# Attention with V split in two: both halves of V in one 32-column stationary operand, two passes per split step in place of three

## Chip, core and metric

The kernel runs on one core of a Trainium2 chip. The metric is device time in microseconds (us) of one execution. "Before" has a median of 1079.02 us over three runs (1078.17 to 1079.59).

## What is computed

Input x has 2048 rows of 512. Two branches are mixed row by row with a gate g = sigmoid(x · gate_w):

```python
q = (x @ wq) as 32 heads of 16;  k = x @ wk;  v = x @ wv      # one k and one v of 16 columns for all heads
a = softmax(q @ k.T / 4) @ v, heads joined, @ wo              # wo: 512 x 512
b = silu(x @ w1) @ w2                                         # w1: 512 x 1792, w2: 1792 x 512
out = g * a + (1 - g) * b
```

All of it is asked for in fp32. The kernel gets there with 16-bit products: a number is held as a high half and a low half (fp16 or bf16), and a product is the sum of three 16-bit products, or it is done natively in fp32.

## The kernel before, in words

**Prologue** (`first_pass`, L351 to L489). x is transposed on TensorE and split; k, v, and the first queries are computed. `VF` (L484) holds V in fp32 with 16 dims and a column of ones (column 16, for the softmax sum) in 32 columns per tile of 128 keys. `v_parts` (L332) makes `VH` (fp16 of V) and `VL` (V minus VH). After it, in VectorE's order, come a minimum (`note`, L349), the low half of the second query block (L117), and then the work of the first step of attention. PSUM banks 6 and 7 are the buffers `pm` of the products between.

**Attention** (`attention`, L701). A round is 512 queries (chunk c), an output block o of 128 query columns and a half rb: 32 rounds. A step is one tile of 128 keys of a round: 16 steps per round, 512 in all. The loop (L1067) takes two steps, a pair, at a time, and issues a pair's work in an order written out as a string: `SPLIT`, `NATIVE` or their wide forms (L27).

- **S** (`scores`, L987): eight small matmuls (32 columns each) write scores into a two-bank PSUM tile; there are two of these tiles. Then ScalarE does one exp over 128x1024 (L1000). A step has two S, a pair four.
- **F**: eight matmuls of other products, the feed-forward, the projection of the output or queries (L741), which fill the array. A pair has 6 F, a wide one 12.
- **P** or **N** (`pv`, L1026): probabilities times V, of earlier steps. The even step of the pair before comes as three P (`VH`·upper half, `VL`·upper half, `VH`·lower half) where it is split, or as one native fp32 N. The odd step is always N. In the program a P is 8 matmuls and an N stands in the profile as 16.
- **low** (`low`, L1010): for a split step VectorE takes the upper half (a bf16 view of the fp32 bits) off the probabilities, two instructions of 128x1024 (L1021). They are issued at the third and fourth S of the step's own pair, so before the P that reads them by about a pair. Step 0 of each round and steps under some feed-forward phases are native (`split_step`, L1006).
- **norm_a** (L939): after a round's last N the accumulators pv0 and pv1 (one buffer each) are transposed into T and U, added, and divided by column 16. It goes to VectorE's queue ahead of whatever the next pair issues. `norm_b` and `norm_c` (L952, L956) finish a pair of rounds, and `out_proj` uses the result.
- **The planner** (`spend`, `put`, `fill`, L750 to L779): each pair has room for 3.7 us of VectorE work (4.1 or 4.95 in two cases). Work that cannot be moved is booked with `spend` (1.15 per low, 2.4 for a norm_a, 0.68 for an eviction of a product); what can wait (norm_b at 0.65, the split of a hidden block at 1.0, pieces of weights at 1.3, maxima at 1.1) is issued at the end of a pair if it fits in what is left, or when it is due by age.

After the last pair the remaining products run (L1106 on). The last output projection waits for the last round's norm_a, norm_b and norm_c.

**Ranges** (`RANGES`, L39): maxima of the operands are compared with limits; if one lies outside, a second, scaled pass of the whole work follows (L1115).

Of the kernel before, what the change touches and what calls it, by code (L numbers as in the profile page):

```python
# [6 lines left out]
F32 = mybir.dt.float32  # L7
BF = mybir.dt.bfloat16
F16 = mybir.dt.float16
# [4 lines left out]
OP = mybir.AluOpType  # L14
AX = mybir.AxisListType
# [6 lines left out]
NF = max(GF)  # L22
ACCS = 4

SPLIT, NATIVE = "SFFFSFFFSPPPSBN", "SFFFSFFFSNBSN"  # L27
WIDE = {SPLIT: "SFFFFFFSFFFFFFSPPPBSN", NATIVE: "SFFFFFFSFFFFFFSNBSN"}

FIRST = "EEEEEEEEEESEESEEEESEEEESBEEEE"  # L30
AHEAD, EARLY = 2, (4, 5)
# [5 lines left out]
QS = LAM / KS  # L37

RANGES = ((0, 8, 0.5, 7.8), (8, 16, 0.5, 7.8), (16, 23, 1.0, 6e4), (23, 25, 1.0, 6e4), (25, 26, 1.0, 6e4),  # L39
          (26, 27, 1.0, 6e4), (27, 28, 1.0, 6e4), (28, 29, 1.0, 6e4), (29, 30, 1.0, 6e4),  # L40
          (30, 31, -1.0, LIMIT * LAM / ONE), (31, 32, -1.0, 0.5))
M_X, M_1, M_2, M_O, M_Q, M_K, M_V, M_G, M_VV, M_B, M_KK = (r[0] for r in RANGES)

# [2 lines left out]
def kernel(  # L46
# [21 lines left out]
    nc = tc.nc  # L68
# [5 lines left out]
    NKT = S // 128  # L74
# [5 lines left out]
    consts = ctx.enter_context(tc.tile_pool(name="consts", bufs=1))  # L80
# [1 line left out]


    KT = consts.tile([128, S], F16)
    VH = consts.tile([128, NKT, 32], F16)
    VL = consts.tile([128, NKT, 32], F16)
    VF = consts.tile([128, NKT, 32], F32)
    gg = consts.tile([128, NKT], F32)
    g1 = consts.tile([128, NKT], F32)
    xs = consts.tile([128, 2, KD, S], F16)  # L90
# [114 lines left out]
    nc.gpsimd.memset(mxs, 0.0)  # L205
    for q in qb_:
        nc.gpsimd.memset(q, 0.0)
    for t_ in (VH, VL, VF):
        nc.gpsimd.memset(t_, 0.0)
    nc.gpsimd.memset(VH[:, :, 16:17], 1.0)  # L210
    nc.gpsimd.memset(VF[:, :, 16:17], 1.0)

    def masks(cst):
        jp = cst.tile([128, 128], F32)
# [50 lines left out]
    def scales(pool, psum, e, srcs, targets):  # L265

        n = len(targets)
        pt_ = psum.tile([128, 512], F32, name="pk")
        nc.tensor.transpose(pt_[0:n, 0:128], srcs, ident)
        m = pool.tile([8, 1], F32, name="am")  # L270
        nc.vector.tensor_reduce(m[0:n], pt_[0:n, 0:128], axis=AX.X, op=OP.max)
        power(m[0:n], m[0:n])
        d = pool.tile([8, 8], F32, name="ad")
        nc.vector.tensor_scalar(d[0:n, 0:n], ident[0:n, 0:n], m[0:n], None, op0=OP.mult)
        one = pool.tile([8, 128], F32, name="one")
        nc.vector.memset(one, 1.0)
# [52 lines left out]
        nc.vector.tensor_scalar(gg, gg, 1.0, None, op0=OP.add)  # L329
        nc.vector.reciprocal(gg, gg)  # L330

    def v_parts():  # L332
        nc.vector.tensor_copy(VH[:, :, 0:16], VF[:, :, 0:16])
        nc.vector.tensor_tensor(VL[:, :, 0:16], VF[:, :, 0:16], VH[:, :, 0:16], op=OP.subtract)


    qsc = QS / (SX * SQ)
# [13 lines left out]
    def first_pass():  # L351
        with ExitStack() as pro:
            sb = pro.enter_context(tc.tile_pool(name="pro", bufs=1))
            wk_ = pro.enter_context(tc.tile_pool(name="prow", bufs=2))
            ps = pro.enter_context(tc.tile_pool(name="props", bufs=1, space=PSUM))
# [126 lines left out]
            V(2)  # L482
            V(3)
            nc.vector.tensor_copy(VF[:, :, 0:16], pv_[:, :, 0:16])  # L484
            v_parts()
            note()
            for _ in q1:
                pass
# [12 lines left out]
    def second_pass():  # L501
        with ExitStack() as pro:
            sb = pro.enter_context(tc.tile_pool(name="pro", bufs=1))
            wk_ = pro.enter_context(tc.tile_pool(name="prow", bufs=2))
            ps = pro.enter_context(tc.tile_pool(name="props", bufs=2, space=PSUM))
# [10 lines left out]
            for a in range(8):  # L516
                n, h = a // 2, a % 2 * F // 2
# [66 lines left out]
            scales(sb, ps, ev, vm, (2.0 ** 13,))  # L584
            nc.vector.tensor_scalar(VF[:, :, 0:16], pv_[:, :, 0:16], ev[:, 0:1], None, op0=OP.mult)
            v_parts()
# [114 lines left out]
    def attention(ctx, scale_of, t_scale, shifts, split_pieces, chores, q_todo, bounds, early, gates_):  # L701
# [237 lines left out]
        def norm_a(pv, rb, st):  # L939

            T, U = wp.tile([128, 512], F32, name="T"), wp.tile([128, 512], F32, name="U")
            T3, U3 = (t.rearrange("p (a b) -> p a b", b=32) for t in (T, U))
            nc.vector.transpose(T, pv[0])  # L943
            nc.vector.transpose(U, pv[1])  # L944
            nc.vector.tensor_tensor(T3[:, :, 0:17], T3[:, :, 0:17], U3[:, :, 0:17], op=OP.add)  # L945
            r = wp.tile([128, 16, 1], F32, name="rr")
            nc.vector.reciprocal(r, T3[:, :, 16:17])
            if rb == 0:
                st["C"] = wp.tile([128, 16, 32], F32, name="C")
            nc.vector.tensor_tensor(st["C"][:, :, 16 * rb:16 * rb + 16], T3[:, :, 0:16], r.to_broadcast([128, 16, 16]), op=OP.mult)  # L950
# [28 lines left out]
        probs, lows, lq, native = {}, {}, [], set()  # L979
# [43 lines left out]
        def upper(P):  # L1023
            return P.bitcast(BF).rearrange("p h (n two) -> p h n two", two=2)[:, :, :, 1]

        def pv(s, n):  # L1026

            i, k = steps[s]
            if k == 0 and n in (0, 3):
                pvs[i] = [pO.tile([128, 512], F32, name=f"pv{h}") for h in range(2)]  # L1030
            first, last = k == 0 and n in (0, 3), k == NKT - 1
            if n == 3:
                a, b = VF[:, k], probs.pop(s)
            else:
                while n == 2 and lq and lq[0][1] == s:
                    low(*lq.pop(0))
                a = (VH, VL, VH)[n][:, k]
                b = lows.pop(s) if n == 2 else upper(probs[s])
                if n == 2:
                    probs.pop(s)  # L1040
            for j in range(4):
                for h, r in enumerate((lo, hi_)):
                    nc.tensor.matmul(pvs[i][h][32 * j:32 * j + 32], a[r], b[r, j], start=first, stop=last)  # L1043
# [23 lines left out]
        for s in range(0, len(steps) + 2, 2):  # L1067
            on = s < len(steps)
            ending[0] = not on
            if on and steps[s][1] == 0:  # L1070
                i = steps[s][0]
                prefetch(i + 1)
                if q_todo and i % 2 == 0:
                    queue.append(q_todo.pop(0))
            p, more = 2 * s, True
            slots, order = SPLIT, [(s - 2, 0), (s - 2, 1), (s - 2, 2), (s - 1, 3)]
# [68 lines left out]
```

## Time and profile before

| what | value |
|---|---|
| three runs | 1078.17, 1079.02, 1079.59 us |
| profiled execution, first to last instruction (span) | 1075.3 us |
| what lies around the span, against the median of the runs | 3.7 us |
| VectorE busy in 300 to 560 / 820 to 1050 us | 201.21 of 260 / 159.38 of 230 us |
| granted TensorE clock | 0.998 |
| split steps / native steps | 174 / 338 |

The profile page gives no time of its own for the profiled execution besides the span; the 3.7 us are taken as the same for both kernels. Split steps are the 1392 matmuls of one of the three P groups divided by eight, native steps the 5408 fp32 records divided by sixteen. Busy time of TensorE is not a measure of what is left in it, since matmuls overlap and their ends are modelled: the distance between the starts of two passes is. A timeline row gives start, duration, engine, line, operation, tiles, shapes and a count of merged instructions, and in brackets the idle time before it with what ended it.

### The profile page before, as it was taken

The page shows a single profiled execution, that of the slowest core. Times are in us where ns is not written, and L with a number is a line of the kernel's source. Part 1 is how long each engine was busy: PE and PEld are TensorE (multiplying, and loading weights), DVE is VectorE, ACT ScalarE, POOL GpSimd, SP SyncE. Part 2 cuts the span into 40 slices and gives each one's busy share as a digit, 9 for nine tenths or more (in the row PEclk, how much of TensorE's full clock was granted, in tenths as well). Part 3 has the DMA queues.
Part 4 walks back from the last instruction along what each step waited for, and adds up shares of the span by engine and source line. Part 5 has one row for each costly group of instructions (what it writes and reads, how often), then busy time and mean ns, then how long its engine had stood idle before and what let it go on. Part 6 is the DMA issues. An engine that isn't in the chain of part 4 may idle for free.

```text
span 1075.3 us, 65967 instructions
## 1 busy us (share of the span) xinstructions
PE 1057.2 (98%) x31224; PEld 667.5 (62%) x31224; DVE 789.9 (73%) x1082; ACT 1008.6 (94%) x1121; POOL 23.4 (2%) x53
## 2 busy tenths in 40 slices
PE   8999999999999999999999999999999999999996
PEld 5455776766665577677655568677756555555552
DVE  6856986968778786878777697675857767476875
ACT  5799999999999999999999999899989999999992
POOL 2110000000000000000000000000000000000000
PEclk9999999999999999999999999999999999999999
DMA  5311111220001000000000100000000110000001
GB/s 208 115 61 45 49 42 31 61 60 14 11 11 41 32 22 10 17 12 12 22 11 21 37 19 21 22 12 11 20 6 12 31 31 12 11 11 5 11 4 43
DMA packets 20840, 32.95 MB, mean 31 GB/s; under 512 B 5137, under 2 KB 12050, under 8 KB 20562
## 3 DMA queue, kind: packets, MB, share of 16 engines
q1 hardware_dynamic: 17618, 20.46, 5.9%
q0 software_dynamic: 2512, 8.13, 2.6%
q8 instruction: 246, 4.03, 1.5%
q14 instruction: 32, 0.26, 0.1%
q10 hardware_dynamic: 432, 0.07, 0.0%
HBM read 20.12 MB, written 8.52 MB: 27 GB/s over the span
## 4 chain that ended last, share of the span: by engine, by line
PE 89%; DVE 5%; ACT 4%; issue 1%; POOL 0%; POOLq 0%; ACTq 0%
PE pv L1043 35%; PE pm L741 31%; PE S L997 19%; ACT P L1000 4%; DVE L L1021 1%; PE pm L745 1%; PE pt L311 0%; PE pk L126 0%; DVE xs L117 0%; DVE T L943 0%; PE pk L127 0%; PE pk L125 0%; DVE U L944 0%; PE pm L342 0%; DVE T L945 0%
## 5 line engine op out<-in xcount | busy, mean ns | idle before, releaser
L1000 ACT ACTIVATE P<-S 128x1024 f32<-128x1024 f32 x1024 | 963.5, 1051 | 24.6 <-PE S L997 19.4
L997 PE MATMUL S<-qb,KT 50*32 50x512 f16 x8192 | 480.1, 378 | 2.3 <-ACT P L1000 2.2
L1021 DVE TENSOR_TENSOR L<-P 128x1024 f16<-128x1024 f32 x348 | 408.1, 1217 | 8.3 <-ACT P L1000 8.2
L1043 PE MATMUL pv<-P,VF 64*32 64x512 f32 x5408 | 374.8, 589 | 0.0
L997 PEld LDWEIGHTS <-KT 50*32 50x32 f16 x8192 | 188.6, 90 | 193.9 <-issue 126.7
L741 PE MATMUL pm<-w2s,H 64*32 64x512 f16 x5232 | 258.8, 375 | 0.6 <-DVE qx L825 0.2
L741 PE MATMUL pm<-xs,w1s 64*32 64x512 f16 x5376 | 248.5, 375 | 1.1 <-issue 0.6
L741 PEld LDWEIGHTS <-H 64*32 64x32 f16 x5232 | 143.7, 93 | 43.5 <-issue 11.3
L741 PEld LDWEIGHTS <-w1s 64*32 64x32 f16 x5376 | 136.3, 93 | 46.1 <-issue 13.5
L1043 PEld LDWEIGHTS pv<-P,VF 64*32 64x32 f32 x5408 | 125.0, 107 | 30.3 <-issue 8.1
L790 DVE SCALAR_TENSOR_TENSOR e<-e,pm 128x512 f32<-128x512 f32 x56 | 38.5, 687 | 140.3 <-ACT e L789 139.4
L1043 PE MATMUL pv<-P,VH 64*32 64x512 bf16 x1392 | 81.9, 389 | 0.0
L1043 PE MATMUL pv<-L,VH 64*32 64x512 f16 x1392 | 81.4, 374 | 0.0
L1043 PE MATMUL pv<-P,VL 64*32 64x512 bf16 x1392 | 81.4, 385 | 0.0
L741 PE MATMUL pm<-xs,wqs 64*32 64x512 f16 x1152 | 81.1, 375 | 0.0
L1043 PEld LDWEIGHTS <-VH 64*32 64x32 f16 x2784 | 60.7, 92 | 20.4 <-issue 3.8
L741 PE MATMUL pm<-wo_s,O 64*32 64x512 f16 x1440 | 63.3, 375 | 0.0
L943 DVE STREAM_TRANSPOSE T<-pv 128x512 f32<-128x512 f32 x32 | 23.0, 717 | 48.0 <-PE pv L1043 40.4
L722 DVE SCALAR_TENSOR_TENSOR acc<-pm,g,acc 128x512 f32<-128x512 f32 x48 | 35.8, 745 | 26.4 <-PE pm L741 24.6
L741 PEld LDWEIGHTS <-wqs 64*32 64x32 f16 x1152 | 43.6, 93 | 10.1 <-issue 2.8
L121 DVE TENSOR_TENSOR H<-e,H 128x512 f16<-128x512 f32 x56 | 38.8, 693 | 1.9
L789 ACT ACTIVATE e<-pm 128x512 f32<-128x512 f32 x56 | 34.5, 616 | 5.7 <-PE pm L741 5.7
(155 smaller groups left out, 478.9 us busy)
## 6 DMA issues: line engine op xcount, KB each, us to landing
qb<-qd SPq DMA_DIRECT2D x192, 32.0 KB
raw<-in_B_w_dram POOLq DMA_DIRECT2D x23, 256.0 KB, 2.9
xn<-in_A_x_dram SPq DMA_DIRECT2D x8, 512.0 KB
out_dram<-acc SPq DMA_DIRECT2D x16, 256.0 KB
qd<-qx SPq DMA_DIRECT2D x12, 256.0 KB
raw<-in_A_wo_dram POOLq DMA_DIRECT2D x4, 256.0 KB, 3.6
qb<-sh SPq DMA_DIRECT2D x62, 2.0 KB
raw<-in_B_w_dram SPq DMA_DIRECT2D x3, 256.0 KB
```

What stands on the lines that cost most here:

```text
L121: nc.vector.tensor_tensor(a2, a, a1, op=OP.subtract)
L722: nc.vector.scalar_tensor_tensor(a, po, gate[:, n:n + 1], a, op0=OP.mult, op1=OP.add)
L741: nc.tensor.matmul(self.bank[32 * m:32 * m + 32], l(i, rows, 32 * m), r(j, rows), start=first, stop=last)
L745: nc.tensor.matmul(self.bank, l(i, slice(0, 128), 0, 128), r(j, slice(0, 128)), start=first, stop=last)
L789: nc.scalar.activation(e, ph, AF.Tanh, scale=t_scale)
L790: nc.vector.scalar_tensor_tensor(e, e, 1.0, ph, op0=OP.add, op1=OP.mult)
L943: nc.vector.transpose(T, pv[0])
L997: nc.tensor.matmul(sc[32 * m:32 * m + 32, f], KT[b:b + 50, k0:k0 + 32], qtile[i][b:b + 50, j], start=True, stop=True)
L1000: nc.scalar.activation(P[:, 2 * j:2 * j + 2], sc, AF.Exp, scale=scale_of(c, o))
L1021: nc.vector.tensor_tensor(lows[s][:, q], P[:, q], upper(P)[:, q], op=OP.subtract)
L1043: nc.tensor.matmul(pvs[i][h][32 * j:32 * j + 32], a[r], b[r, j], start=first, stop=last)
```

## The change

`VH` and `VL` become one operand `VP` of 32 columns. Columns 7 to 15 hold the high half of dims 7 to 15, and columns 23 to 31 their low half. Column 16 stays the ones, so dim 0 has no column for its remainder: dims 0 to 6 are rounded to a grid of 4, and what dim 0 loses is written as six base-4 digits, which are added to the grid values of dims 1 to 6 and taken off again in their low columns 17 to 22. A split step is then VP·upper and VP·lower, and norm_a puts the columns together: it adds column 16+d to column d, and dim 0 gets the sum of columns 17 to 22, each times a power of 1/4 (`mu`).

```diff
-SPLIT, NATIVE = "SFFFSFFFSPPPSBN", "SFFFSFFFSNBSN"
-WIDE = {SPLIT: "SFFFFFFSFFFFFFSPPPBSN", NATIVE: "SFFFFFFSFFFFFFSNBSN"}
+SPLIT, NATIVE = "SFFFSFFFSPPSBN", "SFFFSFFFSNBSN"
+WIDE = {SPLIT: "SFFFFFFSFFFFFFSPPBSN", NATIVE: "SFFFFFFSFFFFFFSNBSN"}
...
-    def v_parts():
-        nc.vector.tensor_copy(VH[:, :, 0:16], VF[:, :, 0:16])
-        nc.vector.tensor_tensor(VL[:, :, 0:16], VF[:, :, 0:16], VH[:, :, 0:16], op=OP.subtract)
+    def v_parts(pool):
+        n = 1 + DIGITS
...
+        nc.vector.tensor_copy(VP[:, :, n:16], VF[:, :, n:16])
+        nc.vector.tensor_tensor(VP[:, :, 16 + n:32], VF[:, :, n:16], VP[:, :, n:16], op=OP.subtract)
+        nc.vector.tensor_scalar(R, VF[:, :, 0:n], GRID * MAGIC, None, op0=OP.add)
+        nc.vector.tensor_scalar(flat_(R), flat_(R), GRID * MAGIC, None, op0=OP.subtract)
+        nc.vector.tensor_tensor(r, VF[:, :, 0:n], R, op=OP.subtract)
+        nc.vector.tensor_tensor(J, r, mu.to_broadcast([128, NKT, n]), op=OP.mult)
+        nc.vector.tensor_reduce(flat_(y), J, axis=AX.X, op=OP.add)
+        nc.vector.tensor_scalar(flat_(y), flat_(y), 1.0 / GRID, None, op0=OP.mult)
+        nc.vector.memset(J[:, :, 0:1], 0.0)
+        for d in range(1, n):
+            j = J[:, :, d:d + 1]
+            nc.vector.tensor_scalar(j, y, BASE, MAGIC, op0=OP.mult, op1=OP.add)
+            nc.vector.tensor_scalar(j, j, MAGIC, None, op0=OP.subtract)
+            if d < n - 1:
+                nc.vector.scalar_tensor_tensor(y, y, BASE, j, op0=OP.mult, op1=OP.subtract)
+        nc.vector.scalar_tensor_tensor(VP[:, :, 0:n], J, GRID, R, op0=OP.mult, op1=OP.add)
+        nc.vector.scalar_tensor_tensor(VP[:, :, 17:16 + n], J[:, :, 1:n], -GRID, r[:, :, 1:n], op0=OP.mult, op1=OP.add)
...
-            nc.vector.tensor_tensor(T3[:, :, 0:17], T3[:, :, 0:17], U3[:, :, 0:17], op=OP.add)
+            nc.vector.tensor_tensor(T, T, U, op=OP.add)
+            z = U3[:, :, 0:DIGITS]
+            nc.vector.tensor_tensor(z, T3[:, :, 17:17 + DIGITS], mu[:, :, 1:].to_broadcast([128, 16, DIGITS]), op=OP.mult)
+            nc.vector.tensor_tensor(T3[:, :, 1:16], T3[:, :, 1:16], T3[:, :, 17:32], op=OP.add)
+            nc.vector.tensor_reduce(U3[:, :, 16:17], z, axis=AX.X, op=OP.add)
+            nc.vector.tensor_tensor(T3[:, :, 0:1], T3[:, :, 0:1], U3[:, :, 16:17], op=OP.add)
...
-                while n == 2 and lq and lq[0][1] == s:
+                while n == 1 and lq and lq[0][1] == s:
...
-                a = (VH, VL, VH)[n][:, k]
-                b = lows.pop(s) if n == 2 else upper(probs[s])
+                a = VP[:, k]
+                b = lows.pop(s) if n else upper(probs[s])
...
-                spend(2.4)
+                spend(3.1)
```

Beside this: the fills of `VH` and `VL` on GpSimd at the start become one of a column of ones and seven of `mu`; the range for the largest |V| becomes 512 to 8000 (it was 1 to 60000); and in the second pass V is scaled to 2^11 rather than 2^13.

More of the change, by code (lines that the diff above doesn't have):

```diff
@@ L23 @@
 ACCS = 4
-SPLIT, NATIVE = "SFFFSFFFSPPPSBN", "SFFFSFFFSNBSN"
-WIDE = {SPLIT: "SFFFFFFSFFFFFFSPPPBSN", NATIVE: "SFFFFFFSFFFFFFSNBSN"}
+GRID, DIGITS, BASE, MAGIC = 4.0, 6, 4.0, 1.5 * 2.0 ** 23
+SPLIT, NATIVE = "SFFFSFFFSPPSBN", "SFFFSFFFSNBSN"
+WIDE = {SPLIT: "SFFFFFFSFFFFFFSPPBSN", NATIVE: "SFFFFFFSFFFFFFSNBSN"}
 FIRST = "EEEEEEEEEESEESEEEESEEEESBEEEE"
@@ L39 @@
 RANGES = ((0, 8, 0.5, 7.8), (8, 16, 0.5, 7.8), (16, 23, 1.0, 6e4), (23, 25, 1.0, 6e4), (25, 26, 1.0, 6e4),
-          (26, 27, 1.0, 6e4), (27, 28, 1.0, 6e4), (28, 29, 1.0, 6e4), (29, 30, 1.0, 6e4),
+          (26, 27, 1.0, 6e4), (27, 28, 1.0, 6e4), (28, 29, 1.0, 6e4), (29, 30, 512.0, 8000.0),
           (30, 31, -1.0, LIMIT * LAM / ONE), (31, 32, -1.0, 0.5))
@@ L84 @@
     KT = consts.tile([128, S], F16)
-    VH = consts.tile([128, NKT, 32], F16)
-    VL = consts.tile([128, NKT, 32], F16)
+    VP = consts.tile([128, NKT, 32], F16)
     VF = consts.tile([128, NKT, 32], F32)
+    mu = consts.tile([128, 1, 1 + DIGITS], F32)
     gg = consts.tile([128, NKT], F32)
@@ L207 @@
         nc.gpsimd.memset(q, 0.0)
[L208 to L211, printed above, removed]
+    nc.gpsimd.memset(VF, 0.0)
+    for t_ in (VP, VF):
+        nc.gpsimd.memset(t_[:, :, 16:17], 1.0)
+    for d in range(1 + DIGITS):
+        nc.gpsimd.memset(mu[:, :, d:d + 1], BASE ** -d if d else -1.0)
     def masks(cst):
@@ L330, in gates @@
         nc.vector.reciprocal(gg, gg)
-    def v_parts():
-        nc.vector.tensor_copy(VH[:, :, 0:16], VF[:, :, 0:16])
-        nc.vector.tensor_tensor(VL[:, :, 0:16], VF[:, :, 0:16], VH[:, :, 0:16], op=OP.subtract)
+    def v_parts(pool):
+        n = 1 + DIGITS
+        R, r, J = (pool.tile([128, NKT, n], F32, name=f"v{q}") for q in "RrJ")
+        y = pool.tile([128, NKT, 1], F32, name="vy")
+        flat_ = lambda t_: t_.rearrange("p a b -> p (a b)")
+        nc.vector.tensor_copy(VP[:, :, n:16], VF[:, :, n:16])
[15 more added lines that the diff above has]
+        nc.vector.scalar_tensor_tensor(VP[:, :, 17:16 + n], J[:, :, 1:n], -GRID, r[:, :, 1:n], op0=OP.mult, op1=OP.add)
     qsc = QS / (SX * SQ)
@@ L484, in first_pass @@
             nc.vector.tensor_copy(VF[:, :, 0:16], pv_[:, :, 0:16])
-            v_parts()
+            v_parts(sb)
             note()
@@ L583, in second_pass @@
             ev = sb.tile([128, 2], F32)
-            scales(sb, ps, ev, vm, (2.0 ** 13,))
+            scales(sb, ps, ev, vm, (2.0 ** 11,))
             nc.vector.tensor_scalar(VF[:, :, 0:16], pv_[:, :, 0:16], ev[:, 0:1], None, op0=OP.mult)
-            v_parts()
+            v_parts(sb)
             sigmoid(pv_, zsc)
@@ L1034, in pv @@
             else:
-                while n == 2 and lq and lq[0][1] == s:
+                while n == 1 and lq and lq[0][1] == s:
                     low(*lq.pop(0))
-                a = (VH, VL, VH)[n][:, k]
-                b = lows.pop(s) if n == 2 else upper(probs[s])
-                if n == 2:
+                a = VP[:, k]
+                b = lows.pop(s) if n else upper(probs[s])
+                if n:
                     probs.pop(s)
@@ L1075, in attention @@
             p, more = 2 * s, True
-            slots, order = SPLIT, [(s - 2, 0), (s - 2, 1), (s - 2, 2), (s - 1, 3)]
+            slots, order = SPLIT, [(s - 2, 0), (s - 2, 1), (s - 1, 3)]
             if s - 2 in native:
```

## The prediction, made before the changed kernel was run

> **What bounds the kernel now.** I read the engines' shares first, then the chain that ended last, then the costliest groups.
>
> ```profile
> PE 1057.2 (98%) x31224; PEld 667.5 (62%) x31224; DVE 789.9 (73%) x1082; ACT 1008.6 (94%) x1121; POOL 23.4 (2%) x53
> ...
> PE 89%; DVE 5%; ACT 4%; issue 1%; POOL 0%; POOLq 0%; ACTq 0%
> ...
> L1000 ACT ACTIVATE P<-S 128x1024 f32<-128x1024 f32 x1024 | 963.5, 1051 | 24.6 <-PE S L997 19.4
> L1043 PE MATMUL pv<-P,VL 64*32 64x512 bf16 x1392 | 81.4, 385 | 0.0
> ```
>
> TensorE (PE) is the chain, but ScalarE (ACT) stands at 94% beside it. So the question is not what a P pass takes on PE, but how far PE lies behind ACT's own pace. The timeline of PE over a split pair near the end shows the first; starts count, not durations.
>
> ```profile
> 1035.15 0.41 PE L997 MATMUL S<-qb,KT 50*32 50x512 f16 x8
> 1035.37 0.84 PE L741 MATMUL pm<-wo_s,O 64*32 64x512 f16 x24
> 1036.02 0.41 PE L997 MATMUL S<-qb,KT 50*32 50x512 f16 x8
> ...
> 1036.89 0.41 PE L997 MATMUL S<-qb,KT 50*32 50x512 f16 x8
> 1037.11 0.42 PE L1043 MATMUL pv<-P,VH 64*32 64x512 bf16 x8
> 1037.34 0.42 PE L1043 MATMUL pv<-P,VL 64*32 64x512 bf16 x8
> 1037.56 0.41 PE L1043 MATMUL pv<-L,VH 64*32 64x512 f16 x8
> 1037.78 0.41 PE L997 MATMUL S<-qb,KT 50*32 50x512 f16 x8
> ...
> 1038.86 0.41 PE L997 MATMUL S<-qb,KT 50*32 50x512 f16 x8
> ...
> 1040.49 0.41 PE L997 MATMUL S<-qb,KT 50*32 50x512 f16 x8 [0.36 <-ACT P L1000]
> ```
>
> A group of eight matmuls starts about 0.22 after the one before (three F and an S in 0.87); the N costs four (1037.78 to 1038.86 is 1.08 with its S). The pair takes 3.71 from S to S: 17 groups. The last row is of the next pair, which has one block of F less: there PE **waits 0.36 us for ACT**. So ACT's pace is close under 3.71. The timeline of ACT gives it:
>
> ```profile
> 311.59 0.60 ACT L789 ACTIVATE e<-pm 128x512 f32<-128x512 f32 x1
> 312.07 7.46 ACT L1000 ACTIVATE P<-S 128x1024 f32<-128x1024 f32 x8
> 319.34 0.68 ACT L789 ACTIVATE e<-pm 128x512 f32<-128x512 f32 x1
> 319.82 37.24 ACT L1000 ACTIVATE P<-S 128x1024 f32<-128x1024 f32 x40
> 356.94 0.61 ACT L789 ACTIVATE e<-pm 128x512 f32<-128x512 f32 x1
> ```
>
> From 312.07 to 319.34 stand eight exps without a gap: 0.909 each, **3.635 per pair**; a tanh adds 0.48 (319.34 to 319.82). The forty from 319.82 to 356.94 take 0.928 each, the pace of PE's 3.71.
>
> **The pass that goes.** A split pair falls to 16 groups, 3.71 - 0.22 = 3.49, and ACT's 3.635 takes over: 0.075 are gained, a third of the pass. The distances between first S of pairs sort them:
>
> ```profile
> L997 PE MATMUL S<-qb,KT x8192: 372/377/388, 38.8 to 1052.4; 50*32 50x512 f16 x200
> ```
>
> Of 256 pairs, 172 in the loop are split. Of the 152 with six F whose exps I could measure, 88 run at PE's 3.71 (3.68 to 3.76), 39 follow a tanh and run at ACT's pace already, and some 25 are late for VectorE's (DVE's) sake. 11 more are wide: 23 groups, 5.0, above ACT's 3.635 + 0.48, so there the whole pass counts. The gain:
>
> - 88 x 0.075 = 6.6
> - 11 x 0.22 = 2.4
> - 29 native pairs without a tanh (18 groups, 3.9) follow pairs in which PE can now run ahead into the second S tile: bounds 0 and the 0.27 above ACT's pace; I take 0.05, since two N in a row soon use up such a lead: 1.5
>
> Together **-10.5**; with the bounds, -8 to -13.
>
> The Trainium skill, in "ScalarE: Activation LUTs", section "What ACT_TABLE_LOAD costs", gives an ACTIVATE with immediates 186 ns + 0.833 ns per element and says that neighbours overlap by about 93 ns: by that, an estimate of 946 ns per exp, 3.78 a pair, the pass would have been free already and the 88 would gain 0. The trace disagrees: 0.909 in the row above.
>
> **v_parts.** The prologue's timelines, of DVE and of PE:
>
> ```profile
> 35.83 0.29 DVE L333 CAST VH<-VF 128x256 f16<-128x256 f32 x1
> 36.15 0.42 DVE L334 TENSOR_TENSOR VL<-VF,VH 128x256 f16<-128x256 f32 x1
> 36.50 0.67 DVE L349 TENSOR_REDUCE um<-s 64x1 f32<-64x512 f16 x1
> 37.35 0.69 DVE L117 SCALAR_TENSOR_TENSOR qs__505<-pq,qs__505 128x512 f16<-128x512 f32 x1 [0.19 <-ACT qs__505 L116]
> 39.76 0.69 DVE L824 TENSOR_SCALAR O<-pm 128x512 f16<-128x512 f32 x1 [1.72 <-PE pm L745]
> 40.49 0.69 DVE L825 SCALAR_TENSOR_TENSOR O<-pm,O 128x512 f16<-128x512 f32 x1
> ...
> 52.40 0.17 DVE L493 TENSOR_SCALAR g<-gg 128x16 f32<-128x16 f32 x1
> 52.60 0.17 DVE L494 TENSOR_SCALAR gg<-gg 128x16 f32<-128x16 f32 x1
> ```
>
> ```profile
> 42.50 0.39 PE L342 MATMUL pm<-qx,kab 64*32 64x512 f16 x2
> ```
>
> Two instructions (0.67, 35.83 to 36.50) become 28. 18 work on 16 elements (17 in the loop over digits) at 0.20 from start to start (52.40 to 52.60): 3.6. Nine work on 96 to 144 elements, between 0.17 for 16 and 0.42 for 256 elements: about 0.31 with the gap, 2.8; a memset, 0.13. Sum 6.5, **+5.9** on DVE. Behind it wait L349, L117, then L824 and L825, which empty the first `pm` bank. L825 would end near 45.1 and not at 41.18. The bound's product L342 needs that bank and sits in PE's order ahead of the next S: it moves from 42.50 to about 45.2. **+2.7** for all that follows, since DVE's slack there (1.72 before L824, 1.3 behind L825) is spent. Bounds: v_parts of 5 to 8 us, +1 to +4. The fills on GpSimd are hidden, since it waits a microsecond for a load further on:
>
> ```profile
> 6.52 0.19 POOL L305 COPY wkv<-gwr 128x4 f32<-128x4 f32 x1 [1.00 <-DMA gwr<-in_gate_w_dram]
> ```
>
> Cost 0; two fills of 0.46 go and eight small ones come, so some 0.3 either way without that cover.
>
> **norm_a.** DVE after the last N of a round, a late one and an early one:
>
> ```profile
> 1029.30 0.45 DVE L945 TENSOR_TENSOR T<-T,U 128x272 f32<-128x272 f32 x1
> 1029.78 0.25 DVE L947 RECIPROCAL rr<-T 128x16 f32<-128x16 f32 x1
> 1030.06 0.43 DVE L950 TENSOR_TENSOR C<-T,rr 128x256 f32<-128x256 f32 x1
> 1030.41 2.35 DVE L1021 TENSOR_TENSOR L<-P 128x1024 f16<-128x1024 f32 x2
> ```
>
> ```profile
> 180.26 0.43 DVE L950 TENSOR_TENSOR C<-T,rr 128x256 f32<-128x256 f32 x1
> 180.72 0.71 DVE L954 STREAM_TRANSPOSE T<-C 128x512 f32<-128x512 f32 x1
> 181.36 0.71 DVE L722 SCALAR_TENSOR_TENSOR acc<-pm,g,acc 128x512 f32<-128x512 f32 x1
> 181.99 4.62 DVE L1021 TENSOR_TENSOR L<-P 128x1024 f16<-128x1024 f32 x4
> ```
>
> ```profile
> L121 DVE TENSOR_TENSOR O<-T,O x16: 691/693/695, 124.9 to 1060.4; 128x512 f16<-128x512 f32 x16
> ```
>
> The add of 272 elements (0.45) becomes one of 512 (0.69 by the row of that size), and there follow ones of 96, 240, 96 and 16 elements: by the slope between 272 and 512, 0.26, 0.41, 0.26, 0.18. Where one needs the other they stand 0.03 apart, where not they overlap by 0.08. Sum 1.75 for 0.45: **+1.3** per round; bounds +1.0 and +1.6.
>
> The row at 1030.41 shows who is behind it: the two lows of the round's first split step. They end at 1032.76, and the second half of the pass that reads them stands at 1033.88 (1033.83 and half a dozen matmuls): slack 1.1. The change takes 0.22 of it (a pass fewer ahead) and 0.08 (a shorter pair), so the lows come 1.3 + 0.3 - 1.1 = 0.5 late. ACT hides some 0.3 of it, when it sets the pace: an S tile is free 1.03 after its exp began, the new S needs 0.5, and the exp is due after 2 x 0.909. About 0.2 is left, in ten such rounds: 2.
>
> At 180.26 a norm_b and an eviction stand between. The low's pass there waits already (slack under 0.1). The planner now books 3.1 of 3.7, 0.65 no longer fits, and norm_b moves behind the lows: 1.3 - 0.7 + 0.3 late, or the full 1.3 + 0.3 less a slack of 0.5 where only an eviction stands there. That is 1.0 on average, 0.7 to 0.8 beyond the cover, in seven rounds: 5.5. In the other 14 the movable work leaves the gap, or no split step follows soon: 0.1 each, 1.5. **+9**; bounds: 1 if the late lows are covered, 18 if ACT hides nothing and the planner moves nothing.
>
> **The end.** The last norm_a has no cover; the output projection waits for it:
>
> ```profile
> 1060.41 1.04 PE L745 MATMUL pm<-wo_s,O 128*128 128x512 f16 x2 [2.21 <-DVE O L120]
> ```
>
> +1.3 - 0.22 (the last pass) = **+1.1**.
>
> **Sum.** -10.5 + 2.7 + 9 + 1.1 = +2.3. On the span of 1075.3 that is 1077.6; with the 3.7 us that the median has above the span, **1081.3 us**.
>
> **Rivals.**
>
> 1. The norm is hidden, and it gets faster. The small instructions overlap and the planner clears the gap, so the lows are late by less than ACT hides. For it: DVE is idle for 27% of the span. Against: ten rounds have a slack of only 1.1. With 1 for the rounds: -10.5 + 2.7 + 1 + 1.1 = -5.7, 1073.3.
> 2. DVE becomes the bound at the round's start. Its place is the pass L·VP of each round's first split step; it decides once the lows come more than the 0.3 late that ACT hides. For it: passes that wait for lows already, as at 180. Against: the planner's 0.7 and the cover. With 18, or with a norm_a 0.3 longer and 15, the sum is +9 to +11: 1088 to 1090.
> 3. ACT is the pace already, and the pass was free: pairs stay at 3.71. For it: ACT's 94%. Against: eight exps without a gap take 7.27, not 7.42. Without the 6.6 the sum is +8.9: 1087.9. The rule of the Trainium skill quoted above would lead here.
> 4. The change doesn't do what it says: the largest |V| leaves its new range and the second pass runs, at about another 1000 us. From the inputs, |V| reaches 3601 in the kernel's scale, between 512 and 8000.
>
> **Chances.** Forecast (1077 to 1085) 0.50, rival 1 0.28, rival 2 0.19, rival 3 0.02, rival 4 under 0.01. About 0.2%, 2.2 us, is what a measurement of this kernel can tell from no change. Faster by more: rival 1 but for its slow end, and a little of the forecast's low end: 0.28. Within: the lower half of the forecast and rival 1's slow end, 0.25. Slower: 0.47. The range takes in the times of rivals 1 to 3: 1072.5 to 1090.
>
> **What would show it.** Right: 16 groups per split pair, S to S at 3.63 and PE waiting for ACT; L342 near 45; norm_a's add to the end of C at 2.5 rather than 1.2; the L·VP pass late once a round, most where an eviction stands between. Wrong: split pairs still at 3.71 (no gain), or under 3.6 (ACT's pace was not its limit); L342 at 42.5; rounds' first split pairs without a wait. Most at risk is the term of +9: it is a difference of a lateness and a cover, both under 1 us.

## The result, and the profile after

The changed kernel takes **1086.24 us** (median of 4 runs, 1085.94 to 1089.70), the kernel before on the same chip 1079.30 (4 runs): ratio **1.0075**, 95% interval 1.0057 to 1.0092, 6.9 us slower. The profiled execution spans 1084.2 us, 8.9 more than before.

The page of the changed kernel: busy times, the chain that ended last, and the groups of the exps and of the pass that is left.

```profile
PE 1052.5 (97%) x29832; PEld 586.7 (54%) x29832; DVE 826.5 (76%) x1236; ACT 1006.8 (93%) x1121; POOL 22.8 (2%) x58
...
PE 50%; ACT 32%; DVE 14%; issue 3%; DMA 0%; another core or an unknown queue 0%; ACTq 0%; POOL 0%; DVEq 0%
...
L1028 ACT ACTIVATE P<-S 128x1024 f32<-128x1024 f32 x1024 | 962.8, 1083 | 34.0 <-PE S L1025 27.8
...
L1071 PE MATMUL pv<-L,VP 64*32 64x512 f16 x1392 | 89.3, 375 | 3.4 <-DVE L L1049 2.6
```

The 1392 matmuls are gone. In the chain TensorE (PE) fell from 89% to 50%, while ScalarE (ACT) rose from 4% to 32% and VectorE (DVE) from 5% to 14%. ACT's own wait for S *rose*, from 19.4 to 27.8 us: S now comes late, and the rows below show for whose sake.

Laid side by side by their exps, the two traces part by +5.4 us in the first round, by +2.0 in the other 31 (losses of some 8.5 and gains of some 6.5) and by +1.35 behind the last exp. The prediction's terms for the same three places are +2.7, -10.5 + 9 = -1.5, and +1.1.

A split pair near the end, on PE's timeline (the columns are those of before):

```profile
1041.62 0.48 PE L1025 MATMUL S<-qb,KT 50*32 50x512 f16 x8
1041.83 1.12 PE L1071 MATMUL pv<-P,VF 64*32 64x512 f32 x16
1042.69 0.48 PE L1025 MATMUL S<-qb,KT 50*32 50x512 f16 x8
...
1044.42 0.48 PE L1025 MATMUL S<-qb,KT 50*32 50x512 f16 x8
1044.64 0.49 PE L1071 MATMUL pv<-P,VP 64*32 64x512 bf16 x8
1044.88 0.48 PE L1071 MATMUL pv<-L,VP 64*32 64x512 f16 x8
1045.28 0.41 PE L1025 MATMUL S<-qb,KT 50*32 50x512 f16 x8
```

From S to S in the same place it is 1045.28 - 1041.62 = 3.66, not 3.71. The two P passes start 0.24 apart, so the S behind them could start at 1045.12; it starts 0.16 later. The rest of the removed 0.22 has turned into a wait.

The start, on DVE and on PE, where the bound's product stands:

```profile
42.04 0.25 DVE L357 SCALAR_TENSOR_TENSOR VP<-vJ,vr 128x96 f16<-128x96 f32 x1
42.21 0.67 DVE L372 TENSOR_REDUCE um<-s 64x1 f32<-64x512 f16 x1
42.81 0.67 DVE L119 SCALAR_TENSOR_TENSOR qs__540<-pq,qs__540 128x512 f16<-128x512 f32 x1
43.41 0.68 DVE L847 TENSOR_SCALAR O<-pm 128x512 f16<-128x512 f32 x1
44.11 0.69 DVE L848 SCALAR_TENSOR_TENSOR O<-pm,O 128x512 f16<-128x512 f32 x1
```

```profile
44.86 0.39 PE L365 MATMUL pm<-qx,kab 64*32 64x512 f16 x2 [2.05 <-DVE O L848]
```

The reduction behind v_parts starts at 42.21 instead of 36.50, and the product at 44.86 instead of 42.50. What nobody had counted follows it. The next rows are the changed kernel's stretches around that idle time (us, then busy time of PE, PEld, DVE, ACT, POOL, the granted clock, DMA share, GB/s):

```profile
42.40:45.90 3.50, 1.45 (x15) 0.51 (x14) 3.47 (x7) 1.21 (x2) 0.00 (x0) 1.00 0.30 95
45.90:52.70 6.80, 6.80 (x84) 2.81 (x90) 6.02 (x10) 3.38 (x4) 1.79 (x3) 0.51 0.61 180
```

PE is busy for only 1.45 of 3.5 us, and then the **granted clock is half** for 6.8 us. (A half window, below, is such a stretch at half the granted clock.) That costs another 3.1 in the round's second pair.

Most of the losses in the rounds stand in the third pair of a round, which comes behind the division of the round before. A late one, in round 11: DVE's division, and PE's row with a wait after it.

```profile
407.20 0.69 DVE L968 TENSOR_TENSOR T<-T,U 128x512 f32<-128x512 f32 x1
...
409.08 0.42 DVE L978 TENSOR_TENSOR C<-T,rr 128x256 f32<-128x256 f32 x1
409.42 0.74 DVE L743 TENSOR_SCALAR acc<-pm,g 128x512 f32<-128x512 f32 x1
410.08 2.35 DVE L1049 TENSOR_TENSOR L<-P 128x1024 f16<-128x1024 f32 x2
```

```profile
410.22 0.37 PE L764 MATMUL pm<-xs,w1s 64*32 64x512 f16 x1 [0.31 <-DVE acc L743]
```

From the add to the end of C it is 2.30 us (407.20 to 409.50), where before 1029.30 to 1030.49 made 1.19: +1.1 per round. Behind it stand the eviction that frees a `pm` bank, and then the lows. Here PE waits for the **eviction**. PE's waits over the whole changed kernel (total, times, longest):

```profile
PE pv L1071 <- DVE L L1049: 2.6, 5, 0.7
PE pm L764 <- DVE acc L745: 2.6, 7, 0.4
...
PE pm L764 <- DVE qx L848: 1.4, 2, 0.8
PE pm L764 <- DVE e L813: 0.7, 3, 0.3
```

### The profile page after: what moved, and what is told of

Read it like the earlier page. It is cut to its first block, busy times and chain, and to the rows that moved or that the text cites. A ratio compares the mean times of both kernels' runs of the same rounds, so it can differ in the third digit from the quotient of the medians.

```text
span 1084.2 us, 63344 instructions
## 1 busy us (share of the span) xinstructions
PE 1052.5 (97%) x29832; PEld 586.7 (54%) x29832; DVE 826.5 (76%) x1236; ACT 1006.8 (93%) x1121; POOL 22.8 (2%) x58
## 4 chain that ended last, share of the span: by engine, by line
PE 50%; ACT 32%; DVE 14%; issue 3%; DMA 0%; another core or an unknown queue 0%; ACTq 0%; POOL 0%; DVEq 0%
ACT P L1028 30%; PE pv L1071 18%; PE pm L764 17%; PE S L1025 11%; DVE L L1049 4%; ACT e L812 1%; DVE T L968 1%; DVE T L966 1%; PE pm L768 1%; DVE U L967 1%; DVE C L978 1%; DVE acc L745 1%; DVE T L971 0%; DMA gwr<-in_gate_w_dram 0%; PE pm L365 0%
## 5 line engine op out<-in xcount | busy, mean ns | idle before, releaser
L1028 ACT ACTIVATE P<-S 128x1024 f32<-128x1024 f32 x1024 | 962.8, 1083 | 34.0 <-PE S L1025 27.8
L1025 PE MATMUL S<-qb,KT 50*32 50x512 f16 x8192 | 460.5, 380 | 3.9 <-ACT P L1028 2.4
L1071 PE MATMUL pv<-P,VF 64*32 64x512 f32 x5408 | 370.1, 591 | 0.0
L1025 PEld LDWEIGHTS <-KT 50*32 50x32 f16 x8192 | 195.3, 90 | 253.7 <-issue 183.5
L764 PEld LDWEIGHTS <-H 64*32 64x32 f16 x5232 | 126.9, 93 | 49.7 <-issue 11.8
L764 PEld LDWEIGHTS <-w1s 64*32 64x32 f16 x5376 | 121.7, 93 | 55.5 <-issue 12.5
L1071 PEld LDWEIGHTS pv<-P,VF 64*32 64x32 f32 x5408 | 112.3, 107 | 31.4 <-issue 7.2
L1071 PE MATMUL pv<-L,VP 64*32 64x512 f16 x1392 | 89.3, 375 | 3.4 <-DVE L L1049 2.6
L1071 PE MATMUL pv<-P,VP 64*32 64x512 bf16 x1392 | 80.3, 388 | 0.0
L1071 PEld LDWEIGHTS <-VP 64*32 64x32 f16 x2784 | 57.8, 93 | 37.6 <-issue 22.1
L745 DVE SCALAR_TENSOR_TENSOR acc<-pm,g,acc 128x512 f32<-128x512 f32 x48 | 35.8, 746 | 21.3 <-PE pm L764 19.4
L764 PEld LDWEIGHTS <-O 64*32 64x32 f16 x1440 | 29.0, 93 | 14.4 <-issue 2.1
```

The costliest lines, as they stand in the source:

```text
L745: nc.vector.scalar_tensor_tensor(a, po, gate[:, n:n + 1], a, op0=OP.mult, op1=OP.add)
L764: nc.tensor.matmul(self.bank[32 * m:32 * m + 32], l(i, rows, 32 * m), r(j, rows), start=first, stop=last)
L1025: nc.tensor.matmul(sc[32 * m:32 * m + 32, f], KT[b:b + 50, k0:k0 + 32], qtile[i][b:b + 50, j], start=True, stop=True)
L1028: nc.scalar.activation(P[:, 2 * j:2 * j + 2], sc, AF.Exp, scale=scale_of(c, o))
```

## The experiments

All ratios are to the kernel before, with 95% intervals.

### The pass alone, and its two companions

Three kernels make a table of four with the changed one: with the short or long v_parts, and with the short or long division.

**pass_alone** has both short:

```diff
+        nc.vector.tensor_copy(VP[:, :, 0:16], VF[:, :, 0:16])
+        nc.vector.tensor_tensor(VP[:, :, 17:32], VF[:, :, 1:16], VP[:, :, 1:16], op=OP.subtract)
...
+            nc.vector.tensor_tensor(T3[:, :, 0:17], T3[:, :, 0:17], U3[:, :, 0:17], op=OP.add)
...
+                spend(2.4)
```

> The changed kernel with both, V's two halves in two instructions and the division of before: of the change only the missing pass is left (dim 0's remainder and the low columns are left out of the result). Theory (the terms add up): 8 us less than the kernel before, 1071.3 us, ratio 0.9926, and the median split pair stays at 3.67 us, because ScalarE's exps set it from there on. Rival (the pass brings nothing, as the exps set the pace already with three passes): 1079 us, ratio 1.000; rival on the other side (0.22 us in each of the 174 split pairs, 38 us): 1041 us, ratio 0.965.

**digits_out** has the first half of this edit, **norm_short** the second.

> The changed kernel with two instructions on V instead of 28: the high half is V in half precision, the low half the remainder of dims 1 to 15; dim 0's remainder is left out of the result. Theory (the 5.4 us that the start lost are the bound's product 2.4 us late, and then 3 us of half clock which the 2.05 us of idle TensorE before it bring): VectorE is back where it was before, the product starts at 42.3 us instead of 44.9, the granted clock stays at 1.0 after it, and the whole is 5.4 us shorter: 1080.8 us, ratio to the kernel before 1.0015. Rival (the half clock is no consequence of the wait): only the 2.4 us come back, the clock row still has its half slice, 1083.8 us, ratio 1.004.

> The changed kernel with the division's VectorE work as it was before the change (one add of 17 columns for the six new instructions, and the planner's price back at 2.4); the low columns are left out of the result. Theory (each round's 1.1 us more on VectorE make the low half of the third pair late, and TensorE waits for it in its pass): the late third pairs are gone, some 8 us over the rounds and 1.1 at the end, 1077 us, ratio 0.998. Rival (the late pairs come from the missing pass itself, because TensorE now reaches the low half 0.22 us sooner, with the division as it was): at most 3 us come back, the third pairs are still late, 1083 to 1085 us, ratio 1.004 to 1.005.

| median us (ratio, interval) | short v_parts | long v_parts |
|---|---|---|
| short division | pass_alone 1072.30 (0.9930, 0.9917 to 0.9944) | norm_short 1075.04 (0.9961, 0.9947 to 0.9974) |
| long division | digits_out 1082.81 (1.0031, 1.0020 to 1.0043) | changed 1086.24 (1.0075, 1.0057 to 1.0092) |

The terms nearly add up. Down the columns the division costs 10.5 and 11.2 us, along the rows v_parts costs 2.7 and 3.4, and the pass alone brings **7.0**. With the short division the change would have been faster (norm_short), so it is the division that loses. The columns agree partly by luck, since half windows fall differently: one profiled execution of each kernel shows 6.83 us of half clock at the start of the changed kernel, 3.41 us in round 23 of digits_out and of norm_short, and none before the last exp in pass_alone.

For digits_out the theory hoped for 5.4 and 3.4 came. Its trace shows 5.6 us back in the first round: the product is at 42.5 and no half clock follows. But it loses 1.9 more than the changed kernel in round 23, the place of the largest scatter (below): there its clock is half from 801.60 to 805.01, and the changed kernel's is not. norm_short gives 11.2 where 9 was expected. 3.1 of its profiled gain are the half clock, which it doesn't have although it keeps the idle time; this speaks against the theory as I had put it, by which idle time brings half clock. The two stretches of norm_short:

```profile
42.40:45.90 3.50, 1.45 (x15) 0.46 (x14) 3.47 (x8) 1.45 (x2) 0.00 (x0) 1.00 0.29 95
45.90:52.70 6.80, 6.80 (x151) 3.61 (x150) 5.97 (x10) 5.72 (x7) 1.79 (x3) 1.00 0.65 179
```

The median split pair of pass_alone is 3.67 us, as the theory said: of the 152 pairs with six F, 77 lie between 3.66 and 3.68, where before 87 lay between 3.70 and 3.72.

### A pass fewer still

**one_pass**: TensorE doesn't read the low halves, while DVE still makes them.

```diff
-SPLIT, NATIVE = "SFFFSFFFSPPSBN", "SFFFSFFFSNBSN"
+SPLIT, NATIVE = "SFFFSFFFSPSBN", "SFFFSFFFSNBSN"
...
-            slots, order = SPLIT, [(s - 2, 0), (s - 2, 1), (s - 1, 3)]
+            slots, order = SPLIT, [(s - 2, 0), (s - 1, 3)]
```

> The changed kernel with the second pass of a split step left out too: VectorE still makes the low halves of the probabilities, but TensorE never reads them, so they are left out of the result. Theory (from two passes on ScalarE's exps set the split pair): the median split pair stays at 3.62 to 3.67 us though TensorE has another 0.22 us less to do; what goes is the wait for late low halves, 8 us, one at the end, and 2.4 in the 11 wide pairs: 1075 us, ratio 0.996. Rival (TensorE still sets the pair with two passes): another 0.22 us in most of the 163 split pairs, 1050 us, ratio 0.973.

1083.92 us, ratio 1.0046 (1.0033 to 1.0059). The first half of the theory holds. PE's rows of a split pair:

```profile
1020.57 0.41 PE L1025 MATMUL S<-qb,KT 50*32 50x512 f16 x8 [0.21 <-ACT P L1028]
...
1023.38 0.41 PE L1025 MATMUL S<-qb,KT 50*32 50x512 f16 x8
1023.60 0.42 PE L1070 MATMUL pv<-P,VP 64*32 64x512 bf16 x8
1024.24 0.41 PE L1025 MATMUL S<-qb,KT 50*32 50x512 f16 x8 [0.21 <-ACT P L1028]
```

1024.24 - 1020.57 = 3.67, the same as with two passes, and the 0.21 saved are a wait for ACT. The rival of 1050 is out.

The second half fell. I expected the late third pairs to vanish with the reader of the lows, and 1075 us; over rounds 1 to 31 one_pass is still 6.0 us behind pass_alone, where the changed kernel is 8.5 behind. So only 2.5 of the 8.5 go with the reader of the lows, and 6.0 stay. PE's waits name what they stand for:

```profile
PE S L1025 <- ACT P L1028: 31.3, 136, 0.5
...
PE pm L365 <- DVE acc L743: 3.8, 4, 1.6
...
PE pm L764 <- DVE acc L745: 2.6, 7, 0.4
```

These are banks of `pm` that DVE empties late, because the evictions stand behind the division and the lows in its order. The changed kernel's own pairs say about the same. Four of them (in rounds 2, 3 and 25) wait for a low and take 3.4 us more than in pass_alone; twelve wait for an eviction and take 5.3 more. At the places of rounds 2 and 3 one_pass waits for an eviction in place of the low, so there removing the reader brings little.

### The long division without the missing pass

**norm_long** is the kernel before, three passes, with the changed norm_a and `spend(3.1)` (and `mu`, which it multiplies by):

```diff
-            nc.vector.tensor_tensor(T3[:, :, 0:17], T3[:, :, 0:17], U3[:, :, 0:17], op=OP.add)
+            nc.vector.tensor_tensor(T, T, U, op=OP.add)
+            z = U3[:, :, 0:DIGITS]
...
-                spend(2.4)
+                spend(3.1)
```

> The kernel before, three passes as they were, with the changed division: six instructions for the one add, and the planner's 3.1 for 2.4 (the low columns are 0). Theory (the 10.5 us that the long division costs in the changed kernel come partly of the missing pass, which uses up 0.3 us of the low halves' slack): fewer and shorter late third pairs than in the changed kernel, some 5 us over the rounds, 1.3 at the end, 1085.5 us, ratio 1.006. Rival (the division costs the same whatever the passes): 1089.8 us, ratio 1.0097.

1088.97 us, ratio 1.0084 (1.0071 to 1.0097): +9.7, the rival's figure. The third pairs of rounds 2 and 3 are late by 1.13 and 1.12 us against the kernel before; in the changed kernel it is 1.17 and 1.13 against pass_alone. That PE comes 0.3 us sooner to the lows shows no part in it.

### The division moved

**norm_later** hands what stands behind the two transposes to the planner, in two pieces:

```diff
-                norm_a(pvs.pop(i), rb, state)
-                spend(3.1)
+                first, second = norm_a(pvs.pop(i), rb, state)
+                spend(1.4)
+                put(1.3, 2, first)
+                put(1.1, 3, second)
...
-                    put(0.65, 3, lambda: (norm_b(state), put(1.0, 3, lambda: norm_c(state, (c, o)))))
+                    put(0.65, 4, lambda: (norm_b(state), put(1.0, 3, lambda: norm_c(state, (c, o)))))
```

> The changed kernel with the division's instructions behind its two transposes handed to the planner as two pieces of 1.3 and 1.1 us, due two and three slots later, so that the low halves of the round's first split step go ahead of them. Nothing is left out. Theory (the third pairs are late because the low halves stand behind the division on VectorE): the third pairs are at 3.67 again, some 8 us come back, the end stays: 1078 us, ratio 0.999. Rival (VectorE has no room for the division anywhere near, so that another low half or another eviction is late in its place): at most 3 us come back, 1083 to 1086 us, ratio 1.004 to 1.0075.

**1076.17 us**, ratio 0.9970 (0.9959 to 0.9982): 10.1 us came back, more than the theory's 8. The profiled execution doesn't meet the half clock at the start, which is 3.1 of it, and the clocks of all six (0.995 to 0.998, in the changed kernel 0.991 to 0.993) say that the others don't either. That leaves 7.0 for the division. DVE in the same round 11:

```profile
400.47 0.73 DVE L743 TENSOR_SCALAR acc<-pm,g 128x512 f32<-128x512 f32 x1
401.12 2.34 DVE L1055 TENSOR_TENSOR L<-P 128x1024 f16<-128x1024 f32 x2
403.39 0.68 DVE L970 TENSOR_TENSOR T<-T,U 128x512 f32<-128x512 f32 x1
...
404.60 2.35 DVE L1055 TENSOR_TENSOR L<-P 128x1024 f16<-128x1024 f32 x2
406.87 0.25 DVE L975 TENSOR_REDUCE U<-U 128x16 f32<-128x96 f32 x1
```

The eviction and the lows go first, the division fills in behind each. Over rounds 1 to 31 it is 1.0 us *ahead* of pass_alone, though it does the whole long division. The 1.0 lies in round 23; without that round the two are level. DVE had the time, not the order.

### The start: stall and clock

**v_long** is the kernel before with the digits' 26 instructions on scratch tiles:

```diff
+        VS = pool.tile([128, NKT, 32], F16, name="vs")
...
+        nc.vector.scalar_tensor_tensor(VS[:, :, 0:n], J, GRID, R, op0=OP.mult, op1=OP.add)
```

> The kernel before with the 26 further instructions of the digits added on scratch tiles at the place where the change has them, so that only the start is longer. Theory (they push the bound's product 2.4 us back; TensorE then stands idle for 2.05 us, and whether a window of half clock follows depends on where the idle time falls): 1081.5 us, ratio 1.002, without a half window near 46 us, or 1084.5 us, ratio 1.005, with one. Rival (VectorE's 5.6 us all reach the end): 1085 us, ratio 1.0052, without any half clock at the start.

1084.37 us, ratio 1.0040 (1.0027 to 1.0054). Its profiled execution loses 2.6 in the first pair and 3.1 in the second, with a half window:

```profile
42.80:46.20 3.40, 1.17 (x14) 0.40 (x5) 3.37 (x7) 1.02 (x1) 0.00 (x0) 1.00 0.28 98
46.20:53.00 6.80, 6.80 (x84) 2.81 (x90) 6.01 (x10) 3.39 (x4) 1.79 (x3) 0.52 0.63 180
```

Of its six executions two took 1081.3 and 1081.7 us at a mean granted clock of 0.996 and 0.997, the other four 1084.3 to 1086.3 at 0.992 to 0.994: the theory's two figures, 1081.5 and 1084.5, both occur. The rival had the median right, but by a way that isn't there.

**pe_busy** fills most of the changed kernel's idle time on PE (0.74 us of the 2.05 are left ahead of the spare products):

```diff
+                    if not s:
+                        spare = pO.tile([128, 512], F32, name="pv1")
+                        for _ in range(9):
+                            nc.tensor.matmul(spare, wqs[:, 0, 0, 0:128], xs[:, 0, 0, 0:512], start=True, stop=True)
```

> The changed kernel with nine spare products of 128x128x512, whose result nobody reads, on TensorE just ahead of the bound's product, in the time in which it stood idle there; VectorE's work and the lateness of the bound's product stay as they are. Theory (the idle time before it causes the half clock): no half clock from 46 to 53 us, so 3 us shorter than the changed kernel, 1083.2 us, ratio 1.0036. Rival (the half clock comes from something else at the start, such as the load of the whole chip): the clock row is as it was and the time 1086.2 us or, if the spare products push the bound's product back, more: ratio 1.0064 to 1.0075.

1087.80 us, ratio 1.0073 (1.0059 to 1.0086): no better. In its trace there is no half window at the start, the second pair has its 3.1 us back, and the product is pushed to 45.94, which costs 0.5. Round 23 then takes 3.0 more than in the changed kernel, with a half window at 805.71. So the clock's part is seen in the profile but not in the time, which leaves this experiment inconclusive as a measure.

### The digits moved

**v_gpsimd** puts the digits' loop and the last writes on GpSimd (POOL):

```diff
...
-            nc.vector.tensor_scalar(j, y, BASE, MAGIC, op0=OP.mult, op1=OP.add)
-            nc.vector.tensor_scalar(j, j, MAGIC, None, op0=OP.subtract)
+            nc.gpsimd.tensor_scalar(j, y, BASE, MAGIC, op0=OP.mult, op1=OP.add)
+            nc.gpsimd.tensor_scalar(j, j, MAGIC, None, op0=OP.subtract)
...
```

> The changed kernel with the digits' loop and the last writes of V's halves on GpSimd (26 instructions there, with three split in two); the first eight instructions stay on VectorE. Nothing is left out. Theory (28 instructions on VectorE ahead of the bound's product cost 2.4 us of standing and, where the idle time falls badly, 3 us of half clock; VectorE has 1.7 us of slack there, which the eight fit into): the product is back at 42.5 us, no half clock near 46, 1082 to 1082.8 us, ratio 1.0025 to 1.0033. Rival (the two engines are in each other's way, or GpSimd's instructions are so slow that the first pass on V at 55 us waits): the start loses 2 us or more as before, 1085 us or more, ratio 1.005.

1089.90 us, ratio 1.0103 (1.0087 to 1.0120), the slowest of all. The first two pairs do get their 5.6 us back. The third loses 6.1. POOL, DVE and PE of v_gpsimd:

```profile
47.90 0.40 POOL L359 TENSOR_TENSOR VP<-vr,vJ 128x96 f16<-128x96 f32 x1
48.24 1.14 POOL L180 DMA_DIRECT2D raw<-in_B_w_dram  x2
```

```profile
51.84 0.43 DVE L197 TENSOR_SCALAR w1s<-raw 128x512 f16<-128x512 f32 x1 [5.13 <-DMA raw<-in_B_w_dram]
52.18 0.68 DVE L198 SCALAR_TENSOR_TENSOR w1s<-raw,w1s 128x512 f16<-128x512 f32 x1
52.78 2.35 DVE L1051 TENSOR_TENSOR L<-P 128x1024 f16<-128x1024 f32 x2
```

```profile
54.05 0.40 PE L1073 MATMUL pv<-L,VP 64*32 64x512 f16 x4 [3.54 <-DVE L L1051]
```

It is a chain of three queues. Two loads of W1 stand on POOL behind the digits; DVE, in order, waits 5.13 us for the first; the low behind it is late; and PE waits 3.54 us for the low. The digits' own result was ready at 48.3, in time. The wait is not all of the 6.1: behind it the clock is half for 3.41 us (the columns are those of the clock rows above).

```profile
54.82:58.23 3.41, 3.04 (x48) 1.42 (x55) 3.31 (x8) 1.02 (x1) 0.00 (x0) 0.50 0.17 60
```

**both_moved** has this and norm_later's edit:

> The changed kernel with both repairs: the digits' loop on GpSimd and the division behind its transposes handed to the planner. Nothing is left out. Theory (the repairs add up, since one acts at the start and the other in the rounds): 1076.2 less the 2.4 of the start, 1073.5 us, ratio 0.9947, with the end 1.3 us longer than before as in the changed kernel. Rival (the repairs are in each other's way, or the first shows only where a half clock followed): 1076 us, ratio 0.997, as with the second repair alone.

1079.52 us, ratio 1.0010 (1.0001 to 1.0019). The rival's 1076 was too kind: beside norm_later the start gains 2.25 and loses 5.7, by the same chain and with a half window behind it too (53.65 to 57.06).

**both_loads** gives the two loads to SyncE:

```diff
-                self.load(nc.gpsimd)
+                self.load(nc.sync if self.todo[:1] in ([6], [7]) else nc.gpsimd)
```

> The kernel with both repairs (the digits' loop on GpSimd, the division behind its transposes handed to the planner), and the two loads of W1 that stood on GpSimd's queue behind the digits issued by SyncE instead. Nothing is left out. Theory (the digits on GpSimd lost 5.7 us in the third pair only because they held up these two loads, for which VectorE, and behind it a low half, and behind that TensorE waited): the third pair of the first round is as before, VectorE no longer waits 5 us for raw, and 1079.5 less 5.7 gives 1073.8 us, ratio 0.995. Rival (SyncE's queue is as full there, or the first pass on V waits for GpSimd's digits themselves): the third pair still loses 2 us or more, 1076 us or more, ratio 0.997 or more, no better than the division's repair alone.

**1073.52 us**, ratio **0.9953** (0.9939 to 0.9966). Nothing is left out, and it is faster than both kernels. DVE's wait for the load is down to 1.81, no half window follows, and the third pair loses 1.1 instead of 5.7. A wait is left: SyncE issues the load at 45.50, behind a store of Q at 45.04.

```profile
48.33 0.43 DVE L197 TENSOR_SCALAR w1s<-raw 128x512 f16<-128x512 f32 x1 [1.81 <-DMA raw<-in_B_w_dram]
```

## Why the prediction was right or wrong

The forecast was 1081.3 and the kernel took 1086.2, inside the range and on the slower side, which had been held the likeliest. It lies above the band of the forecast (to 1085) and below that of rival 2 (from 1088). Term by term:

| term | predicted | measured |
|---|---|---|
| the pass that goes | -10.5 | -7.0 (pass_alone) |
| v_parts | +2.7 | +2.7 and +3.4 (the two rows of the table) |
| division, rounds and end | +9 and +1.1 | +10.5 and +11.2 (the two columns) |

**The pass** is the term that was mis-sized, and the step is "A split pair falls to 16 groups, 3.71 - 0.22 = 3.49, and ACT's 3.635 takes over". ACT does take over: one_pass shows that a further pass less changes nothing. But a pair then measures 3.667, so it gains 0.046 and not 0.075. The medians from S to S by slot, over a hundred pairs, tell why: before they are 0.867, 0.868, 0.893 and 1.079 us, after 0.867, 0.868, 0.856 and 1.075. The slots with three F and with N are PE's work as before; only the slot of the P passes can shrink, and there the S waits for a tile that ACT still reads. The 3.635 came from a stretch behind a tanh, in which the exps stood without a gap. In pass_alone's steady pairs of 3.667 the exps start 0.92, 0.90, 0.90 and 0.94 us apart, and the 0.94 comes when PE has just done an N. 88 x 0.046 make 4.0, where 6.6 were put down. The 11 wide pairs fell from 5.004 to 4.853 (median), 1.7 for 2.4. The native pairs that were to gain 1.5 stayed: 3.952 and 3.957 on average. Together this makes 5.7, near the 5.4 between the two spans (1075.3 and 1069.9); the medians give 7.0. The rule of the Trainium skill, "ScalarE: Activation LUTs", section "What ACT_TABLE_LOAD costs", by which the pass had been free, is out: pass_alone is faster.

**v_parts** was right in its mechanism and its size. The chain L372, L119, L847, L848 came as worked out, and the product at 44.86 was 0.3 sooner than the 45.2 foretold. What the step lacked is the half clock after the idle time, 3.1 us in the executions that meet it.

**The division** came out at its size by a way that was partly another. The instructions took 1.1 us more per round and not 1.3. The lows behind it were late, but the eviction of `pm` banks was late with them, and by one_pass 6.0 of the 8.5 us stay when nobody reads the lows. The prediction counted late lows in seventeen rounds; the trace has PE waiting for a low in four pairs. It named one reader of two, so that the size came out is in part luck. The lost slack of 0.3 that the missing pass should cost counted for nothing (norm_long).

**The end** lost 1.35 behind the last exp, for 1.1 predicted:

```profile
1068.83 1.46 PE L768 MATMUL pm<-wo_s,O 128*128 128x512 f16 x3 [3.33 <-DVE O L122]
```

The wait rose from 2.21 to 3.33, by about what the division is longer. That the whole came so near to 1.1 may be luck: the first stretch of half clock there lasts 6.83 us in this trace and 3.41 in that of before, and v_long, with the short division and a wait of 2.2, loses 1.24 there with 6.83 too. How much of the 1.35 is the clock's is open.

**A place that none of the steps named** is round 23, where the range check's numbers go to memory and back. Before, the write went out at 784.31 and its reader came up on DVE at 796.61. In the changed kernel, which is 6.9 us late by this round, the write goes out at 798.47 and the reader comes up at 802.58. So the write is put off by 7 us more, and the reader is not; the planner, which books more for the division, is the likely reason:

```profile
798.47 0.34 SPq L651 DMA_DIRECT2D md<-raw  x1
806.54 0.23 SPq L656 DMA_DIRECT2D raw<-md  x1
```

```profile
809.17 0.37 DVE L662 TENSOR_REDUCE raw<-raw 1x32 f32<-1x128 f32 x1 [6.59 <-DMA raw<-md]
```

DVE stands for 6.59 us, for 6.7 in digits_out and 7.4 in pe_busy, and not at all in pass_alone and norm_short with the short division. This standing is not what lengthens the round: in norm_later DVE stands for 7.16 us and the round takes 0.2 more than before. Around that time PE and ACT also stop, for up to 2.4 us on PE, in the traces of the other kernels too, and the profile shows no releaser ("issue"). The round's excess over before was 1.3 us in the changed kernel, 1.3 in pass_alone, 2.3 in norm_short, 3.2 in digits_out and 4.3 in pe_busy, one execution each. The last three are those with a half window there, behind 1.80 us or more of idle PE; in norm_short:

```profile
788.54:791.95 3.41, 3.41 (x78) 3.27 (x66) 0.00 (x0) 2.40 (x3) 0.00 (x0) 0.50 0.00 0
```

What stops PE there in the first place is open. It is one reason why differences under 2 us between two of these medians say little.

## What to carry to other kernels

Price a removed instruction in the slot in which it stands: if the work behind it waits for the other engine's tile, only the slot's distance to that engine's pace is gained, and here that was 0.046 us of 0.22. Price an added one by everything that stands behind it in its engine's order, evictions and loads no less than its direct reader. The cheapest repair is order: the same division, put behind the evictions and lows, cost nothing in the rounds, while the digits, moved to an idle engine, cost 6 us through two loads in its queue and the half clock behind the wait.

## What the runs showed of the hardware

**The clock.** Half clock came in stretches of 3.41 us or multiples (6.83 in the changed kernel), on a grid of 3.413 us that runs on through an execution. I cut the traces of all thirteen kernels into these windows and added up PE's idle time in each. Away from the kernels' ends, all seven windows with 1.80 us of idle or more (1.80 to 3.37) were followed by half clock, and none with 1.79 or less was. Two of the seven are the changed kernel's and v_long's at the start, two the waits of v_gpsimd and both_moved, three in round 23. In the changed kernel all 2.05 us fell into one window; in norm_short the same 2.05 were cut by the grid into 1.4 and 0.7, and the clock stayed. This is read off the traces, not set by an experiment; pe_busy, with 0.74 us idle at the start, had no half window there. The Trainium skill, "TensorE: Matmul & The Clock Gate", section "What's actually happening", has such a free-running window of about 3.4 us, which agrees; by its table the clock falls after a whole idle window, and here 1.8 us of one were enough. Behind the last exp the windows were followed by half clock at less, from 1.1 us on (though one with 1.33 was not), which I can't explain.

**GpSimd.** A step of the digits' loop on 16 elements took 0.30 to 0.35 us from start to start (45.06 to 45.40 for one), on DVE 0.22. The four instructions that met DVE's split of `w1s` took 0.47 to 0.59 instead of 0.22 to 0.29.
